# Holding early weight fetches behind the softmax, in a fused attention and MLP kernel

## The chip, the core and the metric

The kernel runs on one core of one Trainium2 chip. The metric is the device time of one execution in microseconds. Before the change three runs gave 738.78, 740.24 and 741.04 us, a median of 740.24. The profiled execution took 740.5 us; its span, from the first to the last instruction, is 738.6 us, so 1.9 us lie around it.

## The reference

Sliding-window attention with four sink keys, for 4 batches, 8 heads, 768 positions and 64 channels; then a two-layer MLP on the 3072 tokens, in float32. The weights arrive as float64.

```python
scores = scale * np.matmul(q, k.transpose(0, 1, 3, 2))
keep = (pos[None, :] < n_sink) | ((rel >= 0) & (rel < window))
a = softmax(np.where(keep, scores, -1e9))      # n_sink 4, window 128
x = np.matmul(a, v)                            # then (B*S, H*D) = (3072, 512)
h = x @ w_in                                   # (512, 2048)
out = np.maximum(0.01 * h, h) @ w_out          # (2048, 512)
```

## The kernel before

**Units.** The tokens are cut into eight units of 384 (half a sequence of one batch; T = 3 tiles of 128). A unit's attention handles eight heads; its MLP runs over 16 slices of the hidden dimension (NFC, index `fc`). Two generators produce instructions: `attention_stream` (L482) and `mlp_stream` (L509). A loop (L574) first draws 70 steps of attention alone, the whole of unit 0 and the start of unit 1. Another (L580) then interleaves the MLP of unit u with the attention of unit u + 1. TensorE (PE) executes in exactly this emitted order. The orders on VectorE (DVE), ScalarE (ACT), GpSimd (POOL) and of the DMA issues on SyncE (SP) come from a scheduler that works from the emission order, dependencies and its own estimate of times; once built, each engine works through its list strictly in order.

**Attention.** For each head and query tile `scores` (L258) makes the score matmul `s`; `softmax_early` (L271, units 0 and 1) masks and reduces it on DVE (L278, result `pe`, row maximum `negm`) and exponentiates on ACT (L280). After three tiles `normalise_early` scales by the reciprocal sum (L283, L284, L290 on DVE in unit 0, L288 on ACT in unit 1). `tail_early` (L333) transposes with PE (L338, L339, L342) into a PSUM bank that `slot` (L326) hands out, and ACT copies it out (L340, L343). `values` (L387) multiplies by v (L407) and adds the sink keys (L411). From unit 2 on operands are split into a high and a low part: queries and keys in `split_head` (L226), values in `split_values` (L238: ACT L245, POOL L246). Inputs of the heads come in tiles `qkn` or `qkraw` (L201) and `vraw` or `vn` with `vsraw` (L214); the buffers of heads 3 and later are those that earlier heads give up.

**Weights.** `load_weights(fc)` (L157) issues the fetch of slice fc of both matrices (`wiraw` by L152, `woraw` by L153, 512 KB each) and the decoding from float64. On DVE there are three instructions per tile (L169, L171, L173) through one PSUM bank, tag "d", into `wif` or `wof`. ACT rounds to the high part (L177), POOL subtracts for the low part (L178). From the fifth tile on a fetch is held until the tile four places earlier has been decoded (DEPTH, L161). The first four have nothing that holds them. Slices 0 and 1 are emitted during the first loop (PRE0, PRED, L577), the rest two slices ahead of the MLP of unit 0 (AHEAD, L517). Later, in units 2 to 5, `check_weights` (L181) fetches every tile once more (`ciraw`, `coraw`) to test its range.

**Banks for transposes.** `slot` alternates between two banks. In phase 0 they are tags "h" and "t"; in phase 1 "t" alone serves; in phase 2 "t" and "d" alternate. Phase 2 begins when all 32 weight tiles have been emitted (L581), which is at slice 13 of unit 0.

**MLP.** Per slice: twelve matmuls `h` (L525); `g` on ACT and DVE (L532, L533); its two parts `gh` (ACT L534) and `gl` (L535); nine matmuls `o` (L546) for the previous slice.

Of the kernel before, what the change touches and what calls it, by code (L numbers as in the profile page):

```python
# [9 lines left out]
F32 = mybir.dt.float32  # L10
F32R = mybir.dt.float32r
I32 = mybir.dt.int32
I8 = mybir.dt.int8
AF = mybir.ActivationFunctionType
ALU = mybir.AluOpType
# [5 lines left out]
P = 128  # L21
# [5 lines left out]
NFC = DF // P  # L27
# [27 lines left out]
PRE = 2  # L55
WARM = 22
DEPTH = 4
PRE0 = 24
PRED = 12
W_LO = 1.125 * 2.0 ** -15  # L60
W_HI = 1.875 * 2.0 ** 16
# [51 lines left out]
def fast_path(ctx, tc, cpool, qk, vu, vs, w_in, w_out, out, ident, wz, lim, masks, tri, diag, negm, wmin, wmax):  # L113
    nc = tc.nc
    wpool = ctx.enter_context(tc.tile_pool(name="wpool", bufs=1))
# [38 lines left out]

    decoded = []

    def load_weights(fc):  # L157
        for nm in ("i", "o"):
            raw = wpool.tile([P, 512, 2], I32, tag=f"w{nm}{fc}", name=f"w{nm}raw{fc}")
            dma = fetch(raw, nm, fc)  # L160
            if len(decoded) >= DEPTH:  # L161
                tc.add_manual_dep(dma.ins, decoded[-DEPTH].ins.name,
                                  mybir.DependencyInfo(mybir.DependencyClass.Sync, mybir.DependencyReason.SCHED_ONLY),
                                  reason="pace")
            top, low = raw[:, :, 1], raw[:, :, 0]
            word = ps_t.tile([P, 512], I32, tag="d", name=f"d{nm}{fc}")
            w = iopool.tile([P, 512], F32, tag="io", name=f"w{nm}f{fc}")
            with tc.issue_after(anchor[0].ins):
                nc.vector.tensor_scalar(out=word, in0=top, scalar1=3, scalar2=0x3FFFFFFF,  # L169
                                        op0=ALU.logical_shift_left, op1=ALU.bitwise_and)  # L170
            nc.vector.scalar_tensor_tensor(out=word, in0=top, scalar=-0x40000000, in1=word,  # L171
                                           op0=ALU.bitwise_and, op1=ALU.bitwise_or)
            decoded.append(nc.vector.scalar_tensor_tensor(out=w.bitcast(I32), in0=low, scalar=29, in1=word,  # L173
                                                          op0=ALU.logical_shift_right, op1=ALU.bitwise_or))
            both = wpool.tile([P, 2, 512], F32R, tag=f"w{nm}{fc}", name=f"w{nm}{fc}")
            hi, lo = both[:, 0, :], both[:, 1, :]
            nc.scalar.copy(out=hi, in_=w)  # L177
            nc.gpsimd.tensor_tensor(out=lo, in0=w, in1=hi.bitcast(F32), op=ALU.subtract)  # L178
            wts[nm, fc] = (hi, lo)

    def check_weights(nm, fc):  # L181
        raw = iopool.tile([P, 512, 2], I32, tag="wraw", name=f"c{nm}raw{fc}", bufs=1)
        fetch(raw, nm, fc)
        mag = iopool.tile([P, 512], F32, tag="io", name=f"mag{nm}{fc}")
        zero = iopool.tile([P, 512], F32, tag="io", name=f"zero{nm}{fc}")
        col = (NFC if nm == "o" else 0) + fc
        nc.scalar.activation(out=mag, in_=raw.bitcast(F32)[:, :, 1], func=AF.Abs,
                             accum_out=wmax[:, col:col + 1])
        nc.gpsimd.tensor_scalar(out=zero, in0=mag, scalar1=0.0, scalar2=None, op0=ALU.is_equal)
        with tc.issue_after(anchor[0].ins):  # L190
            nc.vector.tensor_tensor_reduce(out=zero, in0=mag, in1=zero, scale=1.0, scalar=3.0e38,  # L191
                                           op0=ALU.add, op1=ALU.min, accum_out=wmin[:, col:col + 1])
# [252 lines left out]
    def attend_late(u, h, pend, state):  # L445
        odd = h % 2
        sp = split_head(u, h)
        state = state[h // 2 % 2]
        if not odd:
            state["v"] = split_values(u, h)  # L450
            state["sk"] = apool.tile([P, T, 2, NSK], F32, tag="sk", name=f"sk{u}_{h // 2}")
        load_next(u, h)
        pk = apool.tile([P, T, WM], F32, tag="pk", name=f"pk{u}_{h}", bufs=PKB)
        sk = state["sk"]
        pt = apool.tile([P, 2, 2 * TU], F32R, tag="pt", name=f"pt{u}_{h}")
        state["pt", odd] = pt
        for j in range(T):
            ps = scores(u, h, j, (0, TU + NK[u % 2]), sp)
            softmax(u, h, j, ps, pk[:, j, :])
            yield  # L460
            at = len(pend) - (VSW and j == 0 and not odd and len(pend) > 0)
            pend.insert(at, (0, lambda j=j: tail(u, h, j, pk, pt, sk)))
# [46 lines left out]
    def mlp_stream():  # L509
        po = {}  # L510
        prev = None
        for step in range(NU * NFC + 1):
            u, fc = divmod(step, NFC)
            cur = None
            if u < NU:
                if u == 0:
                    while len(wts) < 2 * min(NFC, fc + 1 + AHEAD):  # L517
                        load_weights(len(wts) // 2)
                wh, wl = wts["i", fc]
                ph = ps_h.tile([P, 512], F32, tag="h", name=f"h{u}_{fc}")  # L520
                for cc in range(NCC):
                    xh, xl = xs[u][cc]
                    cs = slice(cc * P, (cc + 1) * P)
                    for c, (w, x) in enumerate(((wh, xh), (wh, xl), (wl, xh))):
                        nc.tensor.matmul(ph[:, 0:TU], lhsT=w[:, cs], rhs=x, start=cc == 0 and c == 0,  # L525
                                         stop=cc == NCC - 1 and c == 2)
                    if cc < NCC - 1:
                        yield
                g = mpool.tile([P, TU], F32, tag="g", name=f"g{u}_{fc}")
                gh = mpool.tile([P, TU], F32R, tag="gh", name=f"gh{u}_{fc}", bufs=2)  # L530
                gl = mpool.tile([P, TU], F32R, tag="gl", name=f"gl{u}_{fc}", bufs=2)
                nc.scalar.mul(g, ph[:, 0:TU], 0.01)  # L532
                anchor[0] = nc.vector.tensor_tensor(out=g, in0=ph[:, 0:TU], in1=g, op=ALU.max)  # L533
                nc.scalar.copy(out=gh, in_=g)  # L534
                (nc.gpsimd if u == 0 else nc.vector).tensor_tensor(out=gl, in0=g, in1=gh.bitcast(F32), op=ALU.subtract)  # L535
                cur = (u, fc, gh, gl)
                yield
            if prev is not None:
                v, f, gh, gl = prev
                if f == 0:  # L540
                    po = [ps_o.tile([P, 512], F32, tag=f"o{t}", name=f"o{v}_{t}") for t in range(T)]
                wh, wl = wts["o", f]
                for t in range(T):
                    tsl = slice(t * P, (t + 1) * P)
                    for c, (gg, w) in enumerate(((gh, wh), (gh, wl), (gl, wh))):
                        nc.tensor.matmul(po[t], lhsT=gg[:, tsl], rhs=w, start=f == 0 and c == 0,  # L546
                                         stop=f == NFC - 1 and c == 2)
                    if f == NFC - 1:
                        last = v == NU - 1 and t == T - 1
                        ob = iopool.tile([P, 512], F32, tag="wraw" if last else "io", name=f"ob{v}_{t}",  # L550
                                         bufs=1 if last else None)
                        r0 = (v * T + t) * P
                        if last:
                            nc.scalar.copy(out=ob[:, 0:256], in_=po[t][:, 0:256])
                            nc.scalar.dma_start(out=out[r0:r0 + P, 0:256], in_=ob[:, 0:256])
                            nc.vector.tensor_copy(out=ob[:, 256:], in_=po[t][:, 256:])
                            nc.sync.dma_start(out=out[r0:r0 + P, 256:], in_=ob[:, 256:])
                        else:
                            nc.vector.tensor_copy(out=ob, in_=po[t])
                            nc.sync.dma_start(out=out[r0:r0 + P, :], in_=ob)  # L560
                    yield
            prev = cur
            if u == NU - 1 and fc == NFC // 2:
                flags.append(needs_general(nc, cpool, slot(), ident, lim, negm, wmin, wmax))
            if 2 <= u < 6 and fc % 2:
                check_weights("io"[fc // 2 % 2], 4 * (u - 2) + fc // 4)
# [7 lines left out]
    while done < att_steps + LEAD0:  # L574
        done += 1
        next(stream)
        if done >= PRE0 and len(wts) < 2 * min(PRE, (done - PRE0 + 1) // PRED):  # L577
            load_weights(len(wts) // 2)
    phase[0] = 1
    for x, _ in enumerate(mlp_stream()):  # L580
        if len(wts) == 2 * NFC:  # L581
            phase[0] = 2
        due = att_steps + LEAD0 + att_steps * (x + 1) // mlp_steps
        due += min(LEAD - LEAD0, (LEAD - LEAD0) * (x + 1) // mlp_steps)
# [203 lines left out]
```

## Time and profile before

| what | value |
|---|---|
| median of three runs | 740.24 us |
| profiled execution | 740.5 us |
| its span | 738.6 us |
| PE busy | 712.1 us (96%) |
| DVE busy | 547.8 us (74%) |
| ACT busy | 422.6 us (57%) |
| POOL busy | 371.2 us (50%) |
| mean granted TensorE clock | 0.988 |

PE has 26.5 us of the span in which it is not busy. A busy time says nothing of speed: PE also counts as busy while its clock is granted at a half. So the table is read together with the granted clock by stretch, and with the list of what PE waited for.

### The profile page before, as it was taken

How to read it: one execution, taken by the hardware profiler on the slowest of the kernel's cores; microseconds unless marked ns; L12 is line 12 of the kernel's file. 1: busy time of each engine (PE TensorE's matmuls, PEld its weight loads, DVE VectorE, ACT ScalarE, POOL GpSimd, SP SyncE). 2: the span in 40 equal slices, each digit the busy share in tenths (PEclk: the TensorE clock that was granted, in tenths of full speed). 3: DMA queues.
4: the chain of work that ended last, by engine and by line, in shares of the span. 5: the costliest groups of instructions: out<-in, count | busy, mean ns of one | idle time of the engine just before them, and what ended most of it. 6: DMA issues, size and time to landing. Idle time of an engine off the chain costs nothing.

```text
span 738.6 us, 12473 instructions
## 1 busy us (share of the span) xinstructions
PE 712.1 (96%) x3871; PEld 622.7 (84%) x3871; DVE 547.8 (74%) x1749; ACT 422.6 (57%) x1178; POOL 371.2 (50%) x500
## 2 busy tenths in 40 slices
PE   6889999899999999999999999999999999999996
PEld 4547887689999988999988988999988999989995
DVE  6678888656667898888888988888888978733222
ACT  4566666657665566656666566666666565522221
POOL 2025556745555676756657676756566556300000
PEclk9899999999999999999999999999999999999999
DMA  8466667122112333324343343324332221001001
GB/s 295 120 208 199 211 207 231 57 87 73 50 55 69 128 108 110 115 87 157 95 126 109 114 126 123 101 100 138 115 111 94 88 69 41 0 1 43 1 1 48
DMA packets 43755, 77.77 MB, mean 105 GB/s; under 512 B 3616, under 2 KB 26400, under 8 KB 43680
## 3 DMA queue, kind: packets, MB, share of 16 engines
q1 hardware_dynamic: 43536, 76.76, 32.8%
q8 instruction: 33, 0.54, 0.3%
q14 instruction: 42, 0.34, 0.1%
q10 hardware_dynamic: 144, 0.13, 0.1%
HBM read 70.58 MB, written 6.29 MB: 104 GB/s over the span
## 4 chain that ended last, share of the span: by engine, by line
PE 82%; DVE 9%; DMA 3%; ACT 3%; issue 1%; SPq 0%; POOL 0%; ACTq 0%; DVEq 0%
PE h L525 32%; PE o L546 32%; PE v L407 8%; PE s L266 6%; PE t L351 2%; DVE gl L535 2%; DMA qkn<-in_qk 1%; DVE zeroi L191 1%; PE v L411 1%; DVE g L533 1%; DMA vsraw<-in_vs 1%; PE t L338 1%; DVE pe L278 0%; DVE xf L419 0%; DVE pk L311 0%
## 5 line engine op out<-in xcount | busy, mean ns | idle before, releaser
L525 PE MATMUL h<-xh,wi 128*128 128x384 f32 x1024 | 314.5, 354 | 1.5 <-DVE g L533 1.5
L546 PE MATMUL o<-wo,gh 128*128 128x512 f32 x768 | 244.9, 400 | 0.0
L525 PEld LDWEIGHTS h<-xh,wi 128*128 128x128 f32 x1024 | 190.5, 188 | 14.4 <-DVE g L533 2.6
L525 PE MATMUL h<-xl,wi 128*128 128x384 f32 x512 | 172.7, 337 | 0.0
L546 PE MATMUL o<-wo,gl 128*128 128x512 f32 x384 | 151.8, 395 | 0.0
L546 PEld LDWEIGHTS o<-wo,gh 128*128 128x128 f32 x768 | 134.1, 189 | 18.0 <-issue 2.4
L320 POOL TENSOR_SCALAR_AFFINE_SELECT pt<-stg 128x256 fp32r<-128x256 f32 x240 | 101.8, 450 | 83.3 <-DVE stg L359 70.0
L533 DVE TENSOR_TENSOR g<-h,g 128x384 f32<-128x384 f32 x128 | 71.0, 555 | 63.3 <-ACT g L532 61.5
L535 DVE TENSOR_TENSOR gl<-g,gh 128x384 fp32r<-128x384 f32 x112 | 93.4, 834 | 16.7 <-ACT gh L534 15.1
L532 ACT ACTIVATE g<-h 128x384 f32<-128x384 f32 x128 | 62.4, 487 | 73.0 <-PE h L525 72.8
L525 PEld LDWEIGHTS h<-xl,wi 128*128 128x128 f32 x512 | 97.1, 190 | 3.3
L232 POOL TENSOR_TENSOR qksp<-qkraw,qksp 64x392 fp32r<-64x392 f32 (+1 forms) x48 | 58.6, 1221 | 63.6 <-issue 46.7
L305 ACT ACTIVATE pk<-pk,negm 128x128 f32<-128x128 f32 (+1 forms) x144 | 58.0, 403 | 50.4 <-DVE negm L302 49.3
L546 PEld LDWEIGHTS o<-wo,gl 128*128 128x128 f32 x384 | 72.3, 188 | 16.9 <-DVE gl L535 0.3
L534 ACT CAST gh<-g 128x384 fp32r<-128x384 f32 x128 | 65.7, 513 | 32.9 <-DVE g L533 30.3
L266 PEld LDWEIGHTS s<-qksp 128*128 128x128 f32 x288 | 53.5, 189 | 6.2 <-issue 0.2
L266 PE MATMUL s<-qksp 128*128 128x260 f32 (+1 forms) x288 | 56.5, 278 | 0.0
L234 POOL TENSOR_TENSOR qksp<-qkraw,qksp 128x384 fp32r<-128x384 f32 x48 | 53.6, 1116 | 3.6
L358 ACT CAST stg<-t 128x128 fp32r<-128x128 f32 x120 | 30.8, 257 | 41.3 <-PE t L351 32.7
L407 PEld LDWEIGHTS v<-pt,vsp 128*128 128x128 f32 x336 | 45.1, 189 | 5.8 <-issue 3.3
L231 ACT CAST qksp<-qkraw 128x776 fp32r<-128x776 f32 (+1 forms) x48 | 42.8, 892 | 10.4 <-PE s L266 10.1
L311 DVE TENSOR_SCALAR pk<-pk,sm 128x132 f32<-128x132 f32 (+1 forms) x120 | 46.0, 384 | 2.4
(131 smaller groups left out, 1084.1 us busy)
## 6 DMA issues: line engine op xcount, KB each, us to landing
qkraw<-in_qk SPq DMA_DIRECT2D x27, 454.0 KB, 3.2
qkraw<-in_qk SPq DMA_DIRECT2D x26, 388.0 KB, 3.2
wiraw<-in_w_in SPq DMA_DIRECT2D x16, 512.0 KB, 3.8
woraw<-in_w_out SPq DMA_DIRECT2D x16, 512.0 KB, 4.2
ciraw<-in_w_in SPq DMA_DIRECT2D x16, 512.0 KB, 3.8
coraw<-in_w_out SPq DMA_DIRECT2D x16, 512.0 KB, 3.6
out<-ob SPq DMA_DIRECT2D x23, 256.0 KB, 2.0
vraw<-in_vu SPq DMA_DIRECT2D x14, 256.0 KB, 2.7
```

Source lines behind the costliest of these rows:

```text
L232: nc.gpsimd.tensor_tensor(out=sp[D:P, TU:TU + n], in0=raw[D:P, TU:TU + n], in1=sp[D:P, TU:TU + n].bitcast(F32), op=ALU.subtract)
L234: nc.gpsimd.tensor_tensor(out=sp[:, TU + n:2 * TU + n], in0=raw[:, 0:TU], in1=sp[:, 0:TU].bitcast(F32), op=ALU.subtract)
L266: nc.tensor.matmul(ps[:, 0:kn], lhsT=sp[:, off + j * P:off + (j + 1) * P], rhs=sp[:, TU + k0:TU + k0 + kn], start=c == 0, stop=c == len(pa ...
L305: nc.scalar.activation(out=w, in_=w, func=AF.Exp, scale=-1.0, bias=neg, accum_out=sm)
L320: nc.gpsimd.affine_select(out=out, in_=src, pattern=([[0, x]] if x > 1 else []) + [[sign, P]], base=-1 if prev else 0, channel_multiplier= ...
L407: nc.tensor.matmul(out[:, o:o + m], lhsT=l, rhs=r, start=c == 0, stop=c == len(mms) - 1, skip_group_check=True)
L525: nc.tensor.matmul(ph[:, 0:TU], lhsT=w[:, cs], rhs=x, start=cc == 0 and c == 0, stop=cc == NCC - 1 and c == 2)
L532: nc.scalar.mul(g, ph[:, 0:TU], 0.01)
L533: anchor[0] = nc.vector.tensor_tensor(out=g, in0=ph[:, 0:TU], in1=g, op=ALU.max)
L534: nc.scalar.copy(out=gh, in_=g)
L535: (nc.gpsimd if u == 0 else nc.vector).tensor_tensor(out=gl, in0=g, in1=gh.bitcast(F32), op=ALU.subtract)
L546: nc.tensor.matmul(po[t], lhsT=gg[:, tsl], rhs=w, start=f == 0 and c == 0, stop=f == NFC - 1 and c == 2)
```

## The change

Four edits. (1) `load_weights` handles one tile per call instead of a pair, and is called in the first loop at steps 20, 32, 44 and 56 (one tile each) instead of 35 and 47 (two each). (2) Each of the first four fetches, and the first of the later range checks (`ciraw0`), is held until `anchor[0]`, the last softmax reduction (L278) emitted before it, has run. (3) Phase 2 begins with the MLP of unit 1 rather than at slice 13 of unit 0. (4) `split_values` is called at the odd head of a pair instead of the even one.

```diff
-PRE0 = 24
+PRE0 = 8
...
-    def load_weights(fc):
-        for nm in ("i", "o"):
-            raw = wpool.tile([P, 512, 2], I32, tag=f"w{nm}{fc}", name=f"w{nm}raw{fc}")
-            dma = fetch(raw, nm, fc)
-            if len(decoded) >= DEPTH:
-                tc.add_manual_dep(dma.ins, decoded[-DEPTH].ins.name,
-                                  mybir.DependencyInfo(mybir.DependencyClass.Sync, mybir.DependencyReason.SCHED_ONLY),
-                                  reason="pace")
+    def pace(dma, after):
+        tc.add_manual_dep(dma.ins, after.ins.name,
+                          mybir.DependencyInfo(mybir.DependencyClass.Sync, mybir.DependencyReason.SCHED_ONLY),
+                          reason="pace")
+
+    def load_weights():
+        fc, nm = len(wts) // 2, "io"[len(wts) % 2]
+        raw = wpool.tile([P, 512, 2], I32, tag=f"w{nm}{fc}", name=f"w{nm}raw{fc}")
+        dma = fetch(raw, nm, fc)
+        pace(dma, decoded[-DEPTH] if len(decoded) >= DEPTH else anchor[0])
...
     def check_weights(nm, fc):
         raw = iopool.tile([P, 512, 2], I32, tag="wraw", name=f"c{nm}raw{fc}", bufs=1)
-        fetch(raw, nm, fc)
+        dma = fetch(raw, nm, fc)
+        if fc == 0 and nm == "i":
+            pace(dma, anchor[0])
...
-        if not odd:
-            state["v"] = split_values(u, h)
+        if odd:
+            state["v"] = split_values(u, h - 1)
+        else:
...
-        if done >= PRE0 and len(wts) < 2 * min(PRE, (done - PRE0 + 1) // PRED):
-            load_weights(len(wts) // 2)
+        if len(wts) < min(2 * PRE, (done - PRE0) // PRED):
+            load_weights()
     phase[0] = 1
     for x, _ in enumerate(mlp_stream()):
-        if len(wts) == 2 * NFC:
+        if x >= mlp_steps:
             phase[0] = 2
```

The built orders show what this moves. In names, `qkn0_3` is the query and key tile of unit 0, head 3; `s0_4_1` the scores of unit 0, head 4, tile 1; `di1` the bank in which input weights of slice 1 are decoded; the last number only counts buffers. The order on PE is the same in both kernels.

First, SP's queue of DMA issues, shortly after the first inputs. Before:

```order
L152 DMA wiraw0_406<-in_w_in 128x4x256
L153 DMA woraw0_416<-in_w_out 128x1024
L152 DMA wiraw1_494<-in_w_in 128x4x256
L153 DMA woraw1_504<-in_w_out 128x1024
L152 DMA ciraw0_3053<-in_w_in 128x4x256
L201 DMA qkn0_3_215<-in_qk0 128x776
L201 DMA qkn0_4_254<-in_qk0 128x776
L201 DMA qkraw0_5_296<-in_qk0 128x776
```

The same stretch of SP's queue in the changed kernel (its lines are numbered a few higher):

```order
L205 DMA qkn0_3_215<-in_qk0 128x776
L205 DMA qkn0_4_254<-in_qk0 128x776
L205 DMA qkraw0_5_296<-in_qk0 128x776
L218 DMA vraw0_4_334<-in_vu0 128x384
L218 DMA vsraw0_4_335<-in_vs 128x128
L152 DMA wiraw0_317<-in_w_in 128x4x256
L205 DMA qkn0_6_353<-in_qk0 128x776
L205 DMA qkn0_7_405<-in_qk0 128x776
L153 DMA woraw0_395<-in_w_out 128x1024
L218 DMA vn0_6_433<-in_vu0 128x384
L218 DMA vsraw0_6_434<-in_vs 128x128
L152 DMA wiraw2_660<-in_w_in 128x4x256
```

Five weight fetches have left their place ahead of the inputs of head 3; `ciraw0` is gone to unit 2 of the MLP. Fetch `wiraw0` waits for the reduction of `s0_3_1`, `woraw0` for that of `s0_4_2`, `wiraw1` for that of `s0_6_1` and `woraw1` for that of `s1_0_0`; `woraw2`, held by the decoding of `woraw0`, stands directly ahead of `wiraw1`.

Second, DVE at heads 6 and 7 of unit 0, where the second slice's input weights are decoded. Before:

```order
L283 TENSOR_SCALAR sm0_6_455<-sm0_6_455 128x3
L169 TENSOR_SCALAR di1_496<-wiraw1_494 128x512
L284 RECIPROCAL sm0_6_455<-sm0_6_455 128x3
L171 SCALAR_TENSOR_TENSOR di1_496<-wiraw1_494,di1_496 128x512
L290 TENSOR_SCALAR pe0_6_454<-pe0_6_454,sm0_6_455 128x128
L290 TENSOR_SCALAR pe0_6_454<-pe0_6_454,sm0_6_455 128x260 x2
L278 ISA pe0_7_516,negm_65<-s0_7_1_531,wide0_143 128x260
```

In the changed kernel:

```order
L287 TENSOR_SCALAR sm0_6_455<-sm0_6_455 128x3
L288 RECIPROCAL sm0_6_455<-sm0_6_455 128x3
L294 TENSOR_SCALAR pe0_6_454<-pe0_6_454,sm0_6_455 128x128
L294 TENSOR_SCALAR pe0_6_454<-pe0_6_454,sm0_6_455 128x260 x2
L171 TENSOR_SCALAR di1_478<-wiraw1_476 128x512
L282 ISA pe0_7_506,negm_65<-s0_7_1_521,wide0_143 128x260
```

The first decoding instruction of `wiraw1` has moved behind the normalisation of head 6, whose transposes PE needs next, and stands ahead of a reduction of head 7. The tile of slice 0 moves up likewise: its first decoding instruction, which stood behind the reduction of `s0_5_1`, now stands behind that of `s0_4_1`.

Third, ACT where the first split values of unit 2 stand, `ssp2_0`, made from the sink rows `vsraw2_0`. Before:

```order
L177 CAST wo12_1376<-wof12_1372 128x512
L245 CAST ssp2_0_1541<-vsraw2_0_1396 128x2x64
L280 ACTIVATE pe1_7_1399,sm1_7_1400<-pe1_7_1399,negm_65 128x260
L340 COPY pt1_6_1255<-t50_1462 128x256
L340 COPY pt1_6_1255<-t51_1472 128x256
```

In the changed kernel:

```order
L179 CAST wo12_1376<-wof12_1372 128x512
L249 CAST ssp2_0_1696<-vsraw2_0_1396 128x2x64
L284 ACTIVATE pe1_7_1399,sm1_7_1400<-pe1_7_1399,negm_65 128x260
L344 COPY pt1_6_1255<-t50_1462 128x256
L344 COPY pt1_6_1255<-t51_1472 128x256
```

Nothing has moved but the line and buffer numbers.

More of the change, by code (lines that the diff above doesn't have):

```diff
@@ L155, in fast_path @@
     decoded = []
-    def load_weights(fc):
-        for nm in ("i", "o"):
-            raw = wpool.tile([P, 512, 2], I32, tag=f"w{nm}{fc}", name=f"w{nm}raw{fc}")
-            dma = fetch(raw, nm, fc)
-            if len(decoded) >= DEPTH:
-                tc.add_manual_dep(dma.ins, decoded[-DEPTH].ins.name,
-                                  mybir.DependencyInfo(mybir.DependencyClass.Sync, mybir.DependencyReason.SCHED_ONLY),
-                                  reason="pace")
[L165 to L179, printed above, removed]
@@ new lines, in pace @@
+    def pace(dma, after):
[7 more added lines that the diff above has]
+        pace(dma, decoded[-DEPTH] if len(decoded) >= DEPTH else anchor[0])
+        top, low = raw[:, :, 1], raw[:, :, 0]
+        word = ps_t.tile([P, 512], I32, tag="d", name=f"d{nm}{fc}")
+        w = iopool.tile([P, 512], F32, tag="io", name=f"w{nm}f{fc}")
+        with tc.issue_after(anchor[0].ins):
+            nc.vector.tensor_scalar(out=word, in0=top, scalar1=3, scalar2=0x3FFFFFFF,
+                                    op0=ALU.logical_shift_left, op1=ALU.bitwise_and)
+        nc.vector.scalar_tensor_tensor(out=word, in0=top, scalar=-0x40000000, in1=word,
+                                       op0=ALU.bitwise_and, op1=ALU.bitwise_or)
+        decoded.append(nc.vector.scalar_tensor_tensor(out=w.bitcast(I32), in0=low, scalar=29, in1=word,
+                                                      op0=ALU.logical_shift_right, op1=ALU.bitwise_or))
+        both = wpool.tile([P, 2, 512], F32R, tag=f"w{nm}{fc}", name=f"w{nm}{fc}")
+        hi, lo = both[:, 0, :], both[:, 1, :]
+        nc.scalar.copy(out=hi, in_=w)
+        nc.gpsimd.tensor_tensor(out=lo, in0=w, in1=hi.bitcast(F32), op=ALU.subtract)
+        wts[nm, fc] = (hi, lo)
@@ L576, in fast_path @@
         next(stream)
-        if done >= PRE0 and len(wts) < 2 * min(PRE, (done - PRE0 + 1) // PRED):
-            load_weights(len(wts) // 2)
+        if len(wts) < min(2 * PRE, (done - PRE0) // PRED):
+            load_weights()
     phase[0] = 1
     for x, _ in enumerate(mlp_stream()):
-        if len(wts) == 2 * NFC:
+        if x >= mlp_steps:
             phase[0] = 2
```

## The prediction

> **What bounds the kernel now.** I read the granted clock by core first, then PE's waits by stretch, then the stretches in which PE stood still or ran slowly, and last the timeline there. The span:
>
> ```profile
> core 0: 738.6 us, clock 0.988
> ```
>
> What PE waited for, longest first (total, times, longest one), from 0 to 70 us:
>
> ```profile
> PE t L342 <- DVE pe L290: 6.2, 4, 2.1
> PE s L266 <- DMA qkn<-in_qk: 3.2, 1, 3.2
> ```
>
> and from 70 to 200 us:
>
> ```profile
> PE t L338 <- DVE wof L173: 3.4, 1, 3.4
> PE t L338 <- ACT pt L340: 0.9, 1, 0.9
> ```
>
> Busy time by stretch (PE, PEld, DVE, ACT, POOL, each with its count), then granted clock, DMA share and GB/s:
>
> ```profile
> 15.00:20.00 5.00, 2.07 (x6) 1.25 (x7) 1.59 (x8) 1.03 (x5) 0.19 (x1) 0.82 0.72 278
> 20.00:25.00 5.00, 5.00 (x16) 3.22 (x15) 1.20 (x4) 1.62 (x5) 0.00 (x0) 0.50 0.17 52
> 45.00:50.00 5.00, 2.57 (x11) 1.47 (x11) 3.40 (x13) 2.85 (x9) 1.41 (x2) 0.89 0.75 225
> 50.00:55.00 5.00, 4.91 (x19) 2.85 (x18) 1.44 (x6) 3.29 (x10) 0.19 (x1) 0.77 0.47 145
> 140.00:160.00 20.00, 16.96 (x80) 14.00 (x81) 9.54 (x32) 10.38 (x29) 9.41 (x11) 0.91 0.11 33
> 300.00:400.00 100.00, 99.91 (x567) 90.28 (x566) 85.68 (x287) 63.65 (x184) 61.69 (x81) 1.00 0.34 108
> ```
>
> In the steady part PE is busy for 99.91 of 100 us at full clock, so a microsecond that PE gains before it should arrive at the end whole. The clock is lost in three places, each time after a wait: 15 to 25 us, 45 to 55 and 140 to 160.
>
> The first place, in the timeline (start, duration, idle time before in brackets):
>
> ```profile
> 6.09 0.38 SPq L152 DMA_DIRECT2D wiraw<-in_w_in  x1
> ...
> 8.10 0.92 SPq L152 DMA_DIRECT2D ciraw<-in_w_in  x1
> ...
> 9.12 2.41 SPq L201 DMA_DIRECT2D qkn<-in_qk  x2
> ...
> 17.93 0.60 PE L266 MATMUL s<-qkn 128*128 128x128 f32 x2 [3.25 <-DMA qkn<-in_qk]
> ...
> 24.89 0.44 PE L266 MATMUL s<-qkn 128*128 128x128 f32 x2
> ...
> 28.23 0.39 PE L266 MATMUL s<-qkraw 128*128 128x128 f32 x2
> ```
>
> and the time from issue to landing of what was issued between 5 and 10 us (count, size, median):
>
> ```profile
> woraw<-in_w_out SPq DMA_DIRECT2D x2, 512.0 KB, 7.0
> ciraw<-in_w_in SPq DMA_DIRECT2D x1, 512.0 KB, 8.8
> qkn<-in_qk SPq DMA_DIRECT2D x1, 388.0 KB, 8.8
> ```
>
> Five weight fetches of 512 KB are issued at 6.09 to 9.02 us, and the input of head 3 at 9.12 stands behind them: 8.8 us to landing. PE waits 3.25 us for it and then works at half clock: head 3 to head 4 takes 24.89 - 17.93 = 6.96 us, head 4 to head 5, at full clock, 28.23 - 24.89 = 3.34.
>
> **The early fetches, what goes.** In the changed queue nothing of weights stands ahead of head 3's input. It is issued by about 9 us at the latest, when head 0's scores have read its buffer. Inputs that land without such a queue:
>
> ```profile
> qkn<-in_qk SPq DMA_DIRECT2D x2, 454.0 KB, 3.2
> ```
>
> (issued from 30 to 45 us.) So it is there by 12.3, and PE asks for it at 17.93 - 3.25 = 14.68. The 3.25 us go, and the slow head shrinks by 6.96 - 3.34 = 3.62. That agrees with the clock: 5 x 0.18 + 5 x 0.50 = 3.4 us of clock lost from 15 to 25. Together 6.87 us at head 4.
>
> **What comes in their place.** The decoding, 12 DVE instructions for four tiles, is as long as before. But DVE is strictly in order, and each first decoding instruction now stands close behind the reduction that releases its own fetch. If the fetch is late, DVE waits, with reductions and normalisations queued behind it, and PE's transposes after those. The cover is the DVE work between the releasing reduction and the decoding. DVE rows before (first pair head 2, second tile and normalisation; then second tiles of heads 3 and 4, third of 4, second of 5; then first and third tile of unit 1, head 0):
>
> ```profile
> 13.51 0.43 DVE L278 CUSTOM_DVE_ANT_0 pe<-s,wide 128x260 f32<-128x260 f32 x1
> 15.98 0.82 DVE L290 TENSOR_SCALAR pe<-pe,sm 128x128 f32<-128x128 f32 x3
> 23.20 0.43 DVE L278 CUSTOM_DVE_ANT_0 pe<-s,wide 128x260 f32<-128x260 f32 x1 [4.22 <-PE s L266]
> 27.23 0.43 DVE L278 CUSTOM_DVE_ANT_0 pe<-s,wide 128x260 f32<-128x260 f32 x1
> 28.04 0.43 DVE L278 CUSTOM_DVE_ANT_0 pe<-s,wide 128x260 f32<-128x260 f32 x1 [0.38 <-PE s L266]
> 31.14 0.43 DVE L278 CUSTOM_DVE_ANT_0 pe<-s,wide 128x260 f32<-128x260 f32 x1 [0.63 <-PE s L266]
> 43.20 0.42 DVE L278 CUSTOM_DVE_ANT_0 pe<-s,wide 128x260 f32<-128x260 f32 x1
> 48.06 0.43 DVE L278 CUSTOM_DVE_ANT_0 pe<-s,wide 128x260 f32<-128x260 f32 x1 [0.77 <-PE s L266]
> ```
>
> Landing of weights, issued from 30 to 45 us (first row) and, two fetches close together, from 56 to 75:
>
> ```profile
> wiraw<-in_w_in SPq DMA_DIRECT2D x2, 512.0 KB, 4.1
> woraw<-in_w_out SPq DMA_DIRECT2D x3, 512.0 KB, 4.7
> ```
>
> Decoding instructions, min/median/max in ns:
>
> ```profile
> L169 DVE TENSOR_SCALAR di<-wiraw x6: 674/691/694, 31.5 to 74.2; 128x512 int32<-128x512 int32 x6
> ```
>
> - Tile `wi0`: from the second tile of head 3 to that of head 4. Cover 3.34 (the full-clock head) to 27.23 - 23.20 = 4.03; landing 4.1 to 4.7. Wait 0.1 to 1.4; I take the middle, 0.7.
> - Tile `wo0`: from the third tile of head 4 past the second of head 5 (31.14 - 28.04 = 3.10), with two decoding instructions (1.4) and head 4's normalisation (0.82) moved in: 5.3, over 4.7. No wait; 1.7 if it landed as late as the 7.0 of the queue above.
> - Tile `wi1`: from the second tile of head 6 to the end of its normalisation, 15.98 + 0.82 - 13.51 = 3.29. Its fetch goes out directly behind `woraw2`, so 4.7 is the nearest landing: 1.4. Bounds 4.1 - 3.29 = 0.8 and 7.0 - 3.29 = 3.7.
> - Tile `wo1`: from the first to the third tile of unit 1's head 0, 48.06 - 43.20 = 4.86, less the three decoding instructions that stood there (2.1): 2.8 to 4.86, against 4.1 to 4.7. Wait 0 to 1.9; I take 0.7.
>
> Together 2.8 us (0.9 to 8.7), so the first stage gains 6.87 - 2.8 = 4.1, with bounds of -1.8 and 6.0. The loss of clock from 45 to 55 us, 5 x 0.11 + 5 x 0.23 = 1.7 us, I leave as it is: it follows waits on saturated DVE, of which the new order has some. If it goes, 1.7 more. On SP every held fetch has issues queued behind it (`wiraw0`: `qkn0_6`; `wiraw1`: `qkn1_1`), but these wait for a third tile's scores of the same head, which come later than the second tile's reduction or with it; I count nothing.
>
> [...]
>
> **The decode bank.** The place around 140 us:
>
> ```profile
> 138.66 0.37 ACT L340 COPY pt<-t 128x256 f32<-128x256 f32 x1
> ...
> 142.29 0.69 DVE L173 SCALAR_TENSOR_TENSOR wof<-woraw,do 128x512 int32<-128x512 int32 x1
> ...
> 143.04 0.33 PE L338 MATMUL t<-ident,pe 128*128 128x128 f32 x1 [3.35 <-DVE wof L173]
> ```
>
> Phase 2 has just begun, and the third transposes of unit 1's head 7 get the bank "d" in which the last tile, `wo15`, is still decoded. PE waits 3.35 us until its last decoding instruction has read it, and the clock then drops: 20 x 0.09 = 1.8 us of it are lost from 140 to 160. With the change these transposes take bank "t", whose reader before, ACT's copy, is over at 139.03, ahead of the 139.69 at which PE asks. So 5.15 us go. What is next late is the same single bank: three more transposes before unit 1's MLP share "t" where they alternated before, and each needs its reader on ACT or DVE to be done. The nearest row of that kind is the 0.9 us wait above; I take 0.5 in all, at most 0.9 x 3 = 2.7. So 4.6 us (2.5 to 5.15).
>
> **The other two edits.** Splitting values at odd heads has moved no row on ACT; the one wait there that PE feels (0.9, above) stays. Zero. `ciraw0` moves to a place just ahead of `coraw0`, and its reader on ACT a few places back; first row where that is, second how long the reader takes (min/median/max, ns):
>
> ```profile
> 249.90 0.34 SPq L153 DMA_DIRECT2D coraw<-in_w_out  x1
> ```
>
> ```profile
> L187 ACT ACTIVATE magi<-ciraw x16: 651/667/673, 249.1 to 560.7; 128x512 f32<-128x512 f32 x16
> ```
>
> In such a stretch DMA is busy a third of the time and ACT for 63.65 of 100 us (last row of the stretches), which hides it. Zero; 4.1 us at worst, if ACT stood for a whole landing and nothing covered it.
>
> **The sum.** 740.5 - 4.1 - 4.6 = 731.8 for the profiled execution, which lies 0.3 above the median of 740.24; against the median 731.5.
>
> **Rivals.**
>
> - The clock also holds from 45 to 55 us. PE's 2.1 us wait there falls away if the normalisation precedes the decoding, as the new order has it at head 6. Against it: that order still pushes head 4's normalisation behind decoding. 731.5 - 1.7 = 729.8. Chance 0.24. [...]
> - DVE's waits for weights eat the first gain: landings of 5.8 us or so rather than 4.1 to 4.7 give, with the covers' middles, 2.1 + 0.5 + 2.5 + 2.0 = 7.1 us of waits against the 6.87. Only the bank remains: 740.24 - 4.6 = 735.6. For it stands that each fetch now starts one head before its use; against it the short DMA queues after 30 us. Chance 0.12.
> - The single "t" bank returns most of the second gain: 731.5 + 2.7 = 734.2. Against it: PE spaces these transposes by whole groups of `h` or `o`. Chance 0.10.
> - Slower. Held fetches land as those at 5 to 10 us did, in 7.0 to 8.8: the four covers, at their middles, sum to 3.7 + 5.3 + 3.3 + 3.8 = 16.1, four landings of 8.0 us to 32, so DVE waits 15.9 us against 6.87 + 4.6 = 11.5 saved: 740.2 + 4.4 = 744.6. It decides from a mean landing of (16.1 + 11.5) / 4 = 6.9 us. Nothing after 30 us landed so late. Chance 0.04.
> - The change doesn't do what it says: the scheduler moved nothing where PE waits, as with the split of values. The rows of SP speak against it, so this would need the gain to be lost in the 70 to 130 us stretch, on DVE. About 740. Chance 0.05.
>
> My forecast keeps 0.45. Range: 727.0 (6.0 + 1.7 + 5.15 = 12.9 gained) to 737.0 (only 3.2 gained, as when bank or fetches fail and a little more). Faster by over 0.3% (2.2 us, about what a measurement of this kernel can tell from no change): 0.90; within it 0.06; slower 0.04.
>
> **What would show it.** The MLP's first matmul before:
>
> ```profile
> 55.74 0.53 PE L525 MATMUL h<-xh,wi 128*128 128x384 f32 x1
> ```
>
> Right: no wait of PE for `qkn` near 15 us and full clock from 15 to 25; this matmul about 4 us earlier, near 51.6; DVE idle for `wiraw` about 1 us ahead of `wi1`'s decoding; no wait of PE for `wof` and full clock where 140 us was; the ACT wait for `vsraw` still there. Wrong: DVE idle for weights by 5 us or more in all; transposes that wait for ACT or DVE on bank "t" by over 2 us; or a steady part in which PE stands more than before.

## The result, and the profile after

The changed kernel takes 733.12 us (median of 7 runs, 732.05 to 734.20), the kernel before 738.17 (7 runs, 736.39 to 741.04). The ratio is 0.9927, with a 95% interval of 0.9905 to 0.9949. The forecast was 731.5, with a range of 727.0 to 737.0.

The profiled execution took 733.14 us. Its span:

```profile
core 0: 731.3 us, clock 0.993
```

From profile to profile the span is 738.6 - 731.3 = 7.3 us shorter; the medians differ by only 5.05. The execution profiled before, at 740.5 us, lay near the upper end of its kernel's runs: beside the experiments below, the kernel before had medians of 736.96 (29 runs), 737.88 (11) and 738.09 (17).

In the changed kernel most helpers stand 4 or 5 lines further down (L278 is L282, L290 is L294, L338 is L342, L525 is L530). PE's waits up to 70 us, then from 70 to 200, then to the end (total, times, longest):

```profile
PE t L346 <- DVE pe L294: 5.8, 4, 2.4
```

```profile
PE t L355 <- DVE pt L363: 1.1, 1, 1.1
PE t L342 <- ACT pt L344: 0.7, 1, 0.7
```

```profile
PE s L270 <- DVE negm L306: 1.1, 1, 1.1
```

The waits for `qkn` (3.2) and for `wof` (3.4) are gone. New are two of 1.1 us, one on bank "t" and one for a reduction late in the program. The stretches (busy time and count of PE, PEld, DVE, ACT, POOL; then granted clock, DMA share, GB/s):

```profile
15.00:20.00 5.00, 5.00 (x27) 3.26 (x25) 3.56 (x19) 3.49 (x14) 0.19 (x1) 1.00 0.59 170
...
25.00:30.00 5.00, 3.22 (x13) 2.14 (x14) 4.86 (x13) 2.83 (x11) 1.45 (x2) 0.82 0.84 270
30.00:35.00 5.00, 4.18 (x19) 2.44 (x18) 2.27 (x11) 2.74 (x9) 1.45 (x2) 0.83 0.70 215
45.00:50.00 5.00, 3.02 (x11) 1.36 (x12) 3.53 (x13) 3.61 (x11) 1.03 (x2) 0.87 0.64 193
50.00:55.00 5.00, 5.00 (x22) 3.93 (x23) 3.43 (x9) 3.43 (x10) 0.69 (x3) 0.79 0.35 109
140.00:160.00 20.00, 18.86 (x100) 15.59 (x100) 11.69 (x45) 11.77 (x34) 10.79 (x17) 1.00 0.28 93
```

The clock is full from 15 to 20 and from 140 to 160 us, as forecast. It still falls from 45 to 55, by 5 x 0.13 + 5 x 0.21 = 1.7 us, as assumed. But it also falls from 25 to 35, by 5 x 0.18 + 5 x 0.17 = 1.75 us, which was not forecast. The timeline of the first stage (start, duration, idle time before in brackets):

```profile
14.43 0.38 PE L270 MATMUL s<-qkn 128*128 128x128 f32 x2
18.12 0.39 PE L270 MATMUL s<-qkn 128*128 128x128 f32 x2
21.69 0.69 DVE L171 TENSOR_SCALAR di<-wiraw 128x512 int32<-128x512 int32 x1 [0.77 <-DMA wiraw<-in_w_in]
25.29 1.26 POOL L180 TENSOR_TENSOR wi<-wif,wi 128x512 fp32r<-128x512 f32 x1 [4.46 <-ACT wi L179]
25.32 1.84 DVE L294 TENSOR_SCALAR pe<-pe,sm 128x128 f32<-128x128 f32 x3
26.78 0.30 PE L346 MATMUL t<-ident,pe 128*128 128x128 f32 x1 [2.35 <-DVE pe L294]
36.84 0.69 DVE L171 TENSOR_SCALAR di<-wiraw 128x512 int32<-128x512 int32 x1 [0.69 <-DMA wiraw<-in_w_in]
44.60 0.69 DVE L171 TENSOR_SCALAR do<-woraw 128x512 int32<-128x512 int32 x1 [1.66 <-DMA woraw<-in_w_out]
51.05 0.72 PE L530 MATMUL h<-xh,wi 128*128 128x384 f32 x1
```

Both kernels issue the same 3871 matmuls in the same order, so the start of a matmul before, less its start after, is what has been gained up to it:

| matmul | before | after | gained | 
|---|---|---|---|
| first score of head 3 | 17.93 | 14.43 | 3.50 |
| first score of head 4 | 24.89 | 18.12 | 6.77 |
| next transposes of `pe` (wait of 2.35) | 30.93 | 26.78 | 4.15 |
| first of the MLP | 55.74 | 51.05 | 4.69 |
| third transposes of unit 1's head 7 | 143.04 | 135.03 | 8.01 |
| some 3 us later | 147.24 | 137.92 | 9.32 |
| transposes on the single bank "t" | 161.05 | 152.84 | 8.21 |
| a score of unit 3's head 3 | 259.50 | 252.69 | 6.81 |

Behind that it lies between 6.7 and 7.2, and at the last matmul at 6.9. The gains come where they were forecast; there are three losses, at 26.8, 152.8 and 252.7 us. The last of these, in the timeline (SPq rows are issues):

```profile
242.44 0.39 SPq L152 DMA_DIRECT2D ciraw<-in_w_in  x1
...
246.13 0.66 ACT L191 ACTIVATE magi<-ciraw 128x512 f32<-128x512 f32 x1 [1.10 <-DMA ciraw<-in_w_in]
246.91 0.33 SPq L153 DMA_DIRECT2D coraw<-in_w_out  x1
251.55 0.67 ACT L191 ACTIVATE mago<-coraw 128x512 f32<-128x512 f32 x1 [2.16 <-DMA coraw<-in_w_out]
252.69 0.48 PE L270 MATMUL s<-qksp 128*128 128x260 f32 x2 [1.14 <-DVE negm L306]
```

ACT, strictly in order, stands still for both range checks, 1.10 and 2.16 us: the first fetch lands 3.7 us after its issue, and the second, which takes the same buffer, can only go out behind it.

### The profile page after: what moved, and what is told of

It reads as the page before. It is cut to its first block, busy times and chain, and to the rows that moved or that the text cites. A ratio compares the mean times of both kernels' runs of the same rounds, so it can differ in the third digit from the quotient of the medians.

```text
span 731.3 us, 12474 instructions
## 1 busy us (share of the span) xinstructions
PE 709.2 (97%) x3871; PEld 619.9 (85%) x3871; DVE 547.3 (75%) x1749; ACT 422.2 (58%) x1178; POOL 370.5 (51%) x500
## 4 chain that ended last, share of the span: by engine, by line
PE 83%; DVE 8%; DMA 4%; ACT 3%; issue 1%; SPq 0%; ACTq 0%; DVEq 0%
PE h L530 33%; PE o L551 33%; PE v L411 8%; PE s L270 6%; PE t L355 2%; DVE gl L540 1%; DMA wiraw<-in_w_in 1%; PE warm L575 1%; DMA woraw<-in_w_out 1%; DVE zeroi L195 1%; DVE g L538 1%; DMA coraw<-in_w_out 1%; DMA vsraw<-in_vs 1%; PE v L415 1%; PE t L342 1%
## 5 line engine op out<-in xcount | busy, mean ns | idle before, releaser
L530 PE MATMUL h<-xh,wi 128*128 128x384 f32 x1024 | 314.5, 354 | 1.3 <-DVE g L538 1.3
L530 PEld LDWEIGHTS h<-xh,wi 128*128 128x128 f32 x1024 | 190.5, 188 | 14.2 <-DVE g L538 2.4
L530 PE MATMUL h<-xl,wi 128*128 128x384 f32 x512 | 172.6, 337 | 0.0
L530 PEld LDWEIGHTS h<-xl,wi 128*128 128x128 f32 x512 | 97.0, 189 | 3.3
```

## The experiments

"Lost clock" is (1 - granted clock) x span, the mean over a kernel's runs: what PE's slow stretches took.

| kernel | median, us (lowest to highest, runs) | ratio to before (95%) | lost clock, us |
|---|---|---|---|
| changed | 733.12 (732.05 to 734.20, 7) | 0.9927 (0.9905 to 0.9949) | 4.7 |
| phase 2 undone | 736.40 (734.64 to 738.97, 12) | 0.9984 (0.9967 to 1.0001) | 5.8 |
| split at even heads | 733.21 (732.31 to 734.44, 6) | 0.9940 (0.9917 to 0.9962) | 4.6 |
| no hold on the first four | 734.89 (732.62 to 738.12, 12) | 0.9974 (0.9957 to 0.9992) | 4.7 |
| before + hold | 734.79 (732.07 to 737.33, 12) | 0.9961 (0.9943 to 0.9979) | 6.8 |
| decoded later | 732.59 (730.13 to 736.82, 6) | 0.9923 (0.9901 to 0.9945) | 5.4 |
| before + hold + bank | 729.70 (728.73 to 731.52, 6) | 0.9890 (0.9870 to 0.9910) | 2.7 |
| the same, phase 2 earlier | 727.92 (727.28 to 728.64, 5) | 0.9861 (0.9841 to 0.9881) | 2.9 |
| first range check fetched earlier | 732.24 (730.64 to 732.70, 6) | 0.9916 (0.9897 to 0.9936) | 4.3 |
| fastest, four fetches free | 729.88 (728.49 to 733.54, 6) | 0.9905 (0.9872 to 0.9938) | 3.5 |
| low part on DVE | 736.94 (734.50 to 737.57, 12) | 0.9980 (0.9961 to 0.9998) | 8.3 |

The kernel before loses 7.0 to 7.1 us of clock in each of its three groups of runs. Of the 4 to 5 us by which the changed kernel is faster, 2.3 are by this measure clock; that the rest is waits follows by subtraction alone. Where matmuls are compared below, this is done as in the table above, profile against profile, so one execution of each stands for its kernel. How far that carries can be seen at the MLP's first matmul: every engine's order up to it is the same in the changed kernel and in experiments 1, 2 and 8, and it starts at 51.05, 52.10, 52.05 and 52.12 us.

**1. Phase 2 undone** (changed kernel).

```diff
-        if x >= mlp_steps:
+        if len(wts) == 2 * NFC:
             phase[0] = 2
```

> The changed kernel with the condition of phase 2 put back to what it was (all 32 weight tiles loaded). My theory: of the changed kernel's 7.3 us the bank is worth 4.9 gross, less the 1.1 us wait on the single bank, so this kernel is 3 to 4 us slower than the changed one, 736 to 737 us; PE waits about 3.4 us for the last decoded tile near 135 us and runs at less than full clock behind it, up to 135 us it stays as the changed kernel is. Rival: the early gain has moved the decoding far enough ahead of the transposes that the bank is free anyway; then it gives 732 to 734 us and no wait of PE for a decoded tile over 1 us.

Measured: 736.40. The wait on the decode bank is back, the same length as before the change:

```profile
138.59 0.47 PE L342 MATMUL t<-ident,pe 128*128 128x128 f32 x1 [3.35 <-DVE wof L175]
```

Against the changed kernel nothing is lost up to this matmul (0.04 us just ahead of it), 6.2 some 5 us behind it (the wait and the clock after it), and 4.9 once the single bank's wait is past: 4.8 net. The clock stayed at half for 6.83 us here and for 3.41 in the kernel before, which makes 1.7 of it; the medians differ by 3.3. The rival, that the earlier decoding has freed the bank anyway, falls.

**2. Values split at even heads again** (changed kernel).

```diff
-        if odd:
-            state["v"] = split_values(u, h - 1)
-        else:
+        if not odd:
+            state["v"] = split_values(u, h)
             state["sk"] = apool.tile(...)
```

> The changed kernel with the values of the late units split at even heads again. My theory: worth nothing, 732.5 to 733.7 us, and the 1.1 us that PE waits near 252 us for a reduction stays, since that comes from the late fetch of the first range check. Rival: that wait comes from the split of values, which stands ahead of the second range check's reader on ACT in the changed kernel; then 731.5 to 732.3 us and no wait there.

Measured: 733.21. In the traces every engine runs the same operations on the same kinds of tile in the same order as in the changed kernel. The matmuls are 1.0 us behind the changed kernel's at the MLP's start and 0.6 at the end, with no step over 0.5 us between, and PE's wait near 252 us stays, at 1.2. This part of the change is worth nothing, and the 1.0 us is what two executions of one order differ by.

**3. No hold** (changed kernel).

```diff
-        pace(dma, decoded[-DEPTH] if len(decoded) >= DEPTH else anchor[0])
+        if len(decoded) >= DEPTH:
+            pace(dma, decoded[-DEPTH])
```

> The changed kernel with the first four weight fetches free to go at the start again (the fetch of the first range check stays held). My theory: four fetches of 512 KB stand ahead of head 3's input again, one fewer than in the kernel before; PE waits 1 to 3.3 us for that input near 15 us, the clock drops behind it (up to 3.4 us more), and the 3.1 us that DVE waits for weights are gone: 733 to 737 us, with the wait for the input back and DVE's gone. Rival: the early gain comes from decoding one tile at a time and not from the hold; then no wait over 0.5 us for that input, and 729 to 731 us.

Measured: 734.89. In the profiled execution PE waits only 0.6 us for `qkn`, and the clock fell before that, so it tells little about the wait. By the matmuls it is 5.0 us behind the changed kernel at 25.5 us and only 0.9 at 50: DVE has no wait for weights left, and the clock is full from 15 us on. Most of what the hold gains early the changed kernel thus gives back before the MLP. The time is as I expected, the wait shorter; experiment 9 asks again on a better base.

**4. The hold alone** (kernel before).

```diff
             if len(decoded) >= DEPTH:
                 tc.add_manual_dep(dma.ins, decoded[-DEPTH].ins.name, ...)
+            else:
+                tc.add_manual_dep(dma.ins, anchor[0].ins.name, ...)
```

> The kernel before with the hold on the first four weight fetches alone: still two tiles at a time, 12 decoding instructions within two heads, later than in the changed kernel. My theory: head 3's input comes in time or with little delay (one fetch of 512 KB, that of the first range check, still stands ahead of it), so up to 6.9 us are gained there; but the decoding waits for each pair's landing with little cover and crowds DVE just ahead of the MLP, so at the MLP's first matmul 1 to 4 us of it are left, and behind it the bank costs 5.2 us as before: 734 to 737.5 us. Rival: the hold does it all, the timing of the decoding nothing; then the MLP's first matmul comes 4.7 us earlier than before, and the time is 733 to 733.8 us plus the bank's 4.9, less 1.4 for the range check, about 735 us, with no more than 3 us of DVE waits for weights.

Measured: 734.79. Timeline rows of DVE and PE, then the stretches:

```profile
29.36 0.69 DVE L173 TENSOR_SCALAR di<-wiraw 128x512 int32<-128x512 int32 x1 [1.09 <-DMA wiraw<-in_w_in]
48.66 0.44 PE L529 MATMUL h<-xh,wi 128*128 128x384 f32 x1 [0.19 <-ACT pt L344]
```

```profile
45.00:50.00 5.00, 3.71 (x18) 2.25 (x18) 2.89 (x11) 4.42 (x16) 0.19 (x1) 1.00 0.81 261
50.00:55.00 5.00, 3.40 (x18) 2.51 (x19) 4.33 (x9) 3.58 (x9) 1.56 (x3) 1.00 0.35 110
```

The time fits both theories, but mine falls for the first stage. With the decoding left late and in pairs, DVE waits 1.1 us for weights in all, the clock stays full up to the MLP, and its first matmul starts at 48.66: 7.1 us earlier than before, where the whole change gains 4.7. The bank then costs what it did. So the other half of the first edit, decoding earlier and singly, costs about 2.4 us. With experiments 6 and 7, whose MLP starts at 48.92 and 48.95, and with the other three executions of the changed kernel's first stage (52.05 to 52.12), it is 2.1 to 3.5.

**5. Decoded later, still singly** (changed kernel): PRE0 from 8 to 29, PRED from 12 to 6. DVE's order in the first stage is then that of experiment 4, only the second and fourth fetches go out later.

> The changed kernel with the same hold, still one tile at a time, but decoded from step 35 to 53 of the attention instead of 20 to 56 (PRE0 29, PRED 6); DVE's order there is that of the kernel with the hold alone, and only the second and the fourth fetch go out later than in that one. Theory A (formed on the runs so far): what costs the changed kernel time early is where the decoding stands, from head 4 on, each tile close behind the reduction that frees its fetch; decoded later it waits less, so the MLP's first matmul comes 1.5 to 2.5 us earlier than the changed kernel's 51.05, DVE waits for weights under 2 us in all, and the time is 730.5 to 732 us. Theory B: it is the splitting into single tiles that costs, since each fetch then has only one head's cover: DVE still waits 3 us or more for weights, the first matmul of the MLP comes at 50.5 or later, 732.5 to 734 us.

Measured: 732.59. Both theories hold for half. From 27 to 42 us this kernel is ahead of the changed one, by 5 us at most and 1.5 at the end (A: the place matters). Then the fourth tile comes late (B: a single fetch has too little cover):

```profile
42.41 0.69 DVE L171 TENSOR_SCALAR do<-woraw 128x512 int32<-128x512 int32 x1 [2.36 <-DMA woraw<-in_w_out]
44.23 1.23 PE L270 MATMUL s<-qkn 128*128 128x260 f32 x2 [3.09 <-DVE negm L282]
```

```profile
45.00:50.00 5.00, 5.00 (x12) 2.21 (x10) 1.21 (x6) 1.65 (x5) 1.26 (x1) 0.50 0.26 70
```

DVE waits, PE behind it, and the clock stays at half for 13.65 us. The profiled execution, at 736.82 us, was the slowest of six; the others took 730.13 to 734.20, so this trace shows the kernel at its worst.

**6. Hold and bank together** (kernel before): experiment 4 with `x >= mlp_steps`.

> The kernel before with two parts of the change alone: the hold on the first four fetches, and phase 2 from the second unit on. Two tiles at a time, values split at even heads, and the fetch of the first range check free at the start, as before. My theory: the two add, 734.8 (hold alone) less what the bank's edit was worth in the run with phase 2 put back (736.4 less 733.1 to 733.2, so 3.2; by the trace 4.1): 730.5 to 731.6 us, faster than the changed kernel; no wait of PE for a decoded tile near 135 us, and none over 1 us near 252 us. Rival: the hold alone moves the decoding to where the bank's edit has nothing to give, or the wait moves to the single bank: 733 us or more.

Measured: 729.70, faster than the changed kernel, which holds more edits. Against experiment 4 the matmuls are 0.3 us behind at the MLP's start, 6.0 ahead at 136 us and 4.25 at the end, so the bank is worth 4.5. Against the changed kernel they are 2.1 us ahead from the MLP's start on and 3.5 from 254 us on, since `ciraw0` goes out at the start here and its reader waits for nothing. From 130 to 150 us the clock is full:

```profile
130.00:150.00 20.00, 19.57 (x106) 16.25 (x104) 11.81 (x42) 12.92 (x38) 13.29 (x14) 1.00 0.11 33
```

**7. Phase 2 some steps earlier** (on top of 6).

```diff
-        if x >= mlp_steps:
+        if x >= mlp_steps - 12:
```

> As the kernel with the hold and the bank's edit, but phase 2 begins 12 steps of the MLP ahead of the second unit, when the last tile has just been decoded. My theory: the 1.1 us that PE waits near 152 us for the reader of the single bank go, since these transposes alternate between the two banks again: 0.8 to 1.3 us less than with the edit as it is, 729.4 to 730.8 us. Rival: the wait is ACT's, which is late there for another reason, and stays: no difference, or a new wait of PE for the last decoded tile.

Measured: 727.92, the fastest here, 10 us below the runs of the kernel before beside it (737.88). All that PE is shown waiting for from 70 to 200 us:

```profile
PE t L342 <- ACT pt L344: 0.5, 1, 0.5
```

The wait on bank "t" is gone, and the matmuls behind 150 us come 1.4 us earlier than in experiment 6.

**8. First range check fetched earlier** (changed kernel).

```diff
         if fc == 0 and nm == "i":
-            pace(dma, anchor[0])
+            pace(dma, decoded[-1])
```

> The changed kernel with the fetch of the first range check held by the last decoding instruction (near 139 us) instead of the last reduction: it goes out some 100 us ahead of its reader, and the second one, which takes the same buffer, a little earlier too. My theory: ACT no longer waits for the first one's landing (1.1 us) and less than 2.2 us for the second, so the 1.1 us that PE waits near 252 us go: 1.0 to 1.5 us less than the changed kernel, 731.6 to 732.2 us. Rival: the wait there comes from elsewhere (the second range check, or DVE's own queue): the same time, and the wait of PE stays.

Measured: 732.24.

```profile
241.53 0.65 ACT L191 ACTIVATE magi<-ciraw 128x512 f32<-128x512 f32 x1
247.99 0.68 ACT L191 ACTIVATE mago<-coraw 128x512 f32<-128x512 f32 x1 [0.45 <-DVE wmin L195]
251.90 0.40 PE L270 MATMUL s<-qksp 128*128 128x260 f32 x2
```

Neither reader waits for a fetch, and PE's wait is gone: against the changed kernel the matmuls are 0.5 us behind up to 251 us and 0.8 ahead at 252, a gain of 1.3 there. The medians differ by 0.9, with intervals of the ratio that overlap, so the trace shows this and the times alone do not.

**9. The four fetches free** (on 7): without the hold, and with `ciraw0` held by `decoded[-1]`.

> The fastest kernel so far (hold on the early fetches, phase 2 early) with that hold undone: the first four weight fetches go out at the start, and only the fetch of the first range check, which the kernel before also had in that queue, is held by the last decoding instruction. Theory A: the hold of the four is worth what the input of head 3 loses to four fetches: PE waits 0.6 to 2 us for it near 15 us and loses up to 1.7 us of clock behind it, while DVE's 1.4 us of waiting for weights go: 728.5 to 731 us against 727.9. Rival B: with the fifth fetch out of the queue the input comes early enough, so the hold of the four gives nothing: no wait of PE over 0.6 us there, full clock from 15 to 25 us, 727 to 728 us.

Measured: 729.88, 2.0 us more than with the hold; the intervals of the two ratios (0.9872 to 0.9938, 0.9841 to 0.9881) just overlap.

```profile
16.91 0.49 PE L270 MATMUL s<-qkn 128*128 128x128 f32 x2 [2.32 <-DMA qkn<-in_qk]
```

```profile
15.00:20.00 5.00, 3.09 (x15) 2.04 (x16) 1.49 (x9) 1.41 (x5) 0.19 (x1) 1.00 0.46 165
```

Theory A holds for the wait: head 3's first score starts at 17.93 behind five fetches, 16.91 behind four, 14.66 to 14.70 behind the range check's alone (experiments 4, 6 and 7) and 14.43 to 15.20 behind none, where the clock was full. The clock did not fall in this execution, behind a wait of 2.32 us; in others of the same kernel, up to 733.54 us, more was lost. By the matmuls this execution is 2.4 us behind experiment 7 at 16 us, 1.0 at the MLP's start and 0.7 at the end, though experiment 7 lost 1.7 us of clock in between and this one none. So the hold saves the wait; how much of the 2.0 us it is worth in the end is not shown clear of the noise.

**10. The low part on DVE** (changed kernel).

```diff
-        nc.gpsimd.tensor_tensor(out=lo, in0=w, in1=hi.bitcast(F32), op=ALU.subtract)
+        (nc.vector if len(decoded) <= 2 * PRE else nc.gpsimd).tensor_tensor(...)
```

> The changed kernel with one thing moved: the subtraction that makes the low part of a weight tile runs on DVE instead of POOL for the first four tiles. It shows whether DVE's normalisations at 25.3 and 40.8 us took 1.84 and 1.82 us instead of 0.82 because POOL's subtraction ran beside them. If so: all normalisations of unit 0 take 0.8 to 0.85 us here, each subtraction adds some 0.5 to 0.7 us to DVE right behind a normalisation, and PE's wait of 2.35 us near 27 us falls to 1.3 or so; the time changes little, 731.5 to 734 us. If not: a normalisation of over 1.2 us stays at the places of wi0 and wi1.

```profile
25.74 0.81 DVE L294 TENSOR_SCALAR pe<-pe,sm 128x128 f32<-128x128 f32 x3
26.16 0.30 PE L346 MATMUL t<-ident,pe 128*128 128x128 f32 x1 [1.28 <-DVE pe L294]
26.46 0.68 DVE L180 TENSOR_TENSOR wi<-wif,wi 128x512 fp32r<-128x512 f32 x1
...
40.09 0.82 DVE L294 TENSOR_SCALAR pe<-pe,sm 128x128 f32<-128x128 f32 x3
...
43.88 1.24 PE L270 MATMUL s<-qkn 128*128 128x260 f32 x2 [1.86 <-DVE negm L282]
```

```profile
45.00:50.00 5.00, 4.75 (x11) 2.21 (x10) 1.89 (x6) 1.38 (x4) 0.00 (x0) 0.50 0.17 62
```

All normalisations take 0.81 or 0.82 us, and PE's wait of 2.35 falls to 1.28: POOL's subtraction had stretched them. The time, 736.94, came out longer than the range expected: DVE now carries four instructions of 0.68 or 0.69, PE waits 1.86 us at 43.88, and the clock stays at half for 13.65 us.

## Why the prediction was right, and where it was wrong

The sign and the range were right, and most places, but the terms did not all come out so, and that 731.5 lies so near the measured 733.12 is in part luck.

- **Head 3's input:** 6.87 us at head 4 forecast, 6.77 found.
- **DVE's waits for weights:** 0.7, 0, 1.4 and 0.7 us, 2.8 in all, were forecast; the rows above have 0.77, 0, 0.69 and 1.66, 3.1 in all. The first MLP matmul was forecast near 51.6 and came at 51.05 (at 52.05 to 52.12 in experiments 1, 2 and 8, with the same order). That sum is right for a partly wrong reason. The failed step is "the decoding ... is as long as before": its place is not free. Moved up, POOL's subtraction met head 4's normalisation, 1.84 us instead of 0.82 (experiment 10), PE waited 2.35 us, and the clock cost 1.75 us more. A second meeting, at 40.78 us, made 1.82 of 0.82. The kernel before had one such meeting, of 1.44 us at 35.63, so the new place adds to a cost that was there. That the MLP still started on time I can't divide further: PE gets some back wherever DVE has been the limit.
- **The clock from 45 to 55 us:** left as it was, and in the profiled execution it fell there. In experiments 1, 2 and 8, whose order up to there is the same, it was full from 45 to 55 us, and at half for 3.41, 6.83 and 6.83 us between 25 and 35 (3.41 in the changed kernel's profile). So the rival that it holds was right in three executions of four, though the 729.8 us that it gives did not come, and that this term came out at 1.7 is luck. With the hold and without the early decoding (experiments 4, 6 and 7) it held there too.
- **The decode bank:** 5.15 us gross forecast, 9.51 - 4.49 = 5.0 found (the gain just ahead of these transposes, and behind the slow stretch that followed them before); undoing it cost 4.8 net in the traces and 3.3 in the medians, adding it to the hold gained 4.5.
- **The single bank "t":** 0.5 forecast, a wait of 1.1 found, and 1.4 gained where experiment 7 takes it away. The rival that it returns 2.7 was right in kind and half the size.
- **The split of values:** 0, and 0 (experiment 2).
- **`ciraw0`:** 0 forecast, a loss of 1.4 found, inside the bound of 4.1. The failed step is "ACT for 63.65 of 100 us, which hides it". A share of busy time says nothing on an engine in order: its reader stood 3.7 us behind the issue, and the second fetch waited for the first one's buffer. Experiment 8 shows it, with 1.3 us regained.
- **The base:** the sum of 8.7 us was set against the 740.24 of three runs. Against the 737 to 738 of the later ones the change gains 4 to 5, from profile to profile 7.3. 731.5 came close to 733.12 because a base that was 2 to 3 us high made up for part of a gain that was forecast too large.

## What to carry to other kernels

Holding a fetch and moving its consumer are two edits: measure them apart, since here the first gained about 7 us by the MLP's start and the second took 2.1 to 3.5 of it. A held fetch needs its cover counted to the reader that stands in order behind it, with the rows of the real landing (3.8 to 4.9 us for these), and the last user of a buffer counts as well. Where executions of one kernel differ by a few microseconds, compare the lost clock before explaining a median, and look for other traces of the same order before explaining one trace.

## What the runs showed of the hardware

- **The clock in steps of 3.41 us.** In the trace's record of the granted clock each half-speed stretch inside the program is a multiple of 3.41 us: 6.83, 3.41 and 3.41 before (from 18.17, 48.89 and 144.46 us); 3.41 twice after (from 28.25 and 48.73); 6.83 in experiment 4; 13.65 in 5; 3.41 and 13.65 in 10; none in 9; 3.41 or 6.83 each in the other six. With a wait of 1.86 us (experiment 10, up to 43.88) the clock fell, with one of 2.32 (experiment 9, up to 16.91) it did not, so its length alone doesn't decide. Counted in steps of 3.41 us from the start of the first full-clock stretch (4.51 us before, 4.36 after), the falls inside the program come at the end of the 4th, 13th and 41st step before, and of the 7th and 13th after. PE was busy for 0.07, 0.43 and 0.42 of the step ahead of the falls before, and for 0.43 and 0.67 after; the least busy step that kept the clock had 0.47 in each of the two traces. Experiments 4 and 6 have the same orders up to 130 us. The 3.41 us from 32.77, first in experiment 4, where the clock stayed full, then in 6, where it was at half for the next 3.41 us:

```profile
32.77:36.18 3.41, 1.73 (x10) 1.19 (x10) 3.24 (x9) 1.60 (x7) 1.46 (x2) 1.00 1.01 371
```

```profile
32.77:36.18 3.41, 1.48 (x9) 1.16 (x9) 3.25 (x9) 1.61 (x6) 1.46 (x2) 1.00 1.04 389
```

  PE was busy for 0.51 of it in experiment 4 and for 0.43 in 6. So here PE's share of such a step goes with the fall, and not sharply: 0.47 kept the clock and 0.67 came ahead of a fall, and the ends of matmuls are modelled.
- **DVE beside POOL.** The three normalisations took 1.84 us instead of 0.82 when POOL's subtraction, 1.26 us long, started 0.03 us ahead of them; alone they took 0.81 or 0.82 each time (experiment 10). The delay was 1.02 us. The one of the three that is stretched ends 0.08 us behind POOL's subtraction at 26.63 (behind 26.55) here, at 36.54 (behind 36.46) in the kernel before and at 34.30 (behind 34.22) in experiment 4, and 0.15 us behind it in the second meeting here, at 42.60 (behind 42.45). Why they meet so, no run shows, and POOL's spans are rough.
